# A decode layer on one core: one weight block moved between DMA engines, the order of the last loads, and transposes on VectorE

## The chip, the core and the metric

The kernel runs on one core of a Trainium2 chip. A core has TensorE (matrix multiply, "PE" in the profile; its weight loads are listed apart as "PEld"), VectorE ("DVE"), ScalarE ("ACT"), GpSimd ("POOL") and SyncE ("SP"), which here only issues DMAs. Sixteen DMA engines move data between HBM and the on-chip memory (SBUF). The metric is device time in microseconds; the runs shown of one kernel lie within 0.03% of each other.

## The reference

A decode step for 8 rows `x` (8 x 512, fp32): attention with 32 query heads over 8 cached key/value heads of 4096 positions and head width 128, and a gated MLP, both on the layer-normalised `x`.

```python
xn = layernorm(x)
q = (xn @ wq)                                   # 32 heads of 128
p = softmax(q @ k_cache^T * 128**-0.5)          # each kv head serves 4 query heads
s = (p @ v_cache) @ wo                          # 4096 x 512
z = gelu(xn @ w_in); z1, z2 = z[:, :896], layernorm(z[:, 896:])
g = silu((z1 * (w_sp * z2 + b_sp)) @ w_out)     # w_out: 896 x 512
out = x + s * g
```

Nearly all bytes are the two caches, 134 MB each; the weights are some 22 MB.

## The kernel before

All large data pass through a ring of three SBUF slots of 64 KB in each of 128 partitions (8 MB a slot). SP issues the loads in program order on one queue: the MLP weights and `w_out` as one transfer (`w_mlp`, L59), `wq` (L74), then for every kv head two key halves (`load_k`, L289) and two value halves (`load_v`, L296), each 8 MB and each issued when the slot it goes into has been read for the last time. `x` comes on ACT's queue (L71). The 128 rows of a transfer are shared out over the 16 DMA engines.

The order of work on the engines is that of the program, with small shifts by the build. First the layer norm of `x` (L121 to L129), then the MLP (`mlp()`: its first product L144, its second, with `w_out` in 7 blocks of 128 rows, L185, its gate, L200), the queries (`project_q`, L207 to L219), then per kv head: `scores` (L230, 64 matmuls a half; each shows as two records in the trace), `softmax` (L237 to L267), and per pair of batch rows `values` (L275) with a masked sum on VectorE (L278, L280) and a small matmul `combine` (L284).

In `softmax` the probabilities `p` (128 x 1024) are transposed by TensorE in 8 blocks (L262) and copied by VectorE in 16 pieces into `pT` (L266). `pT` holds zeros beside each row so that two batch rows can share one 32-column group; `values` then has two batch rows for each result, and four results for a head.

The end of the kernel: after the last key half, the last slot is filled with `wo`, which is 32 blocks of 128 x 512 (256 KB each). Blocks 0 to 11 (`WO_EARLY`) go ahead of the last value half, which comes in two parts, and the other 20 follow in the pieces of `WO_PIECES` (L322). `project_o` multiplies blocks 0 to 27 (`FOLDED`) with the heads' results into `part` (L304); `part` is copied to SBUF (L343) and folded into the 128 x 64 output layout by 16 matmul records (L359). The last four blocks go straight into that layout (`direct`, L351): blocks 28 and 29 ahead of the fold, 30 and 31 (from `AHEAD` on) behind it. Two VectorE operations (L363, L364) and the store (L365) end the kernel. `part` and `acc`, the sum in the output layout, are views of the one PSUM tile `sc`.

Of the kernel before, what the change touches and what calls it, by code (L numbers as in the profile page):

```python
# [8 lines left out]
F32 = mybir.dt.float32  # L9
# [13 lines left out]
NB = FH // P  # L23
EPS = 1e-5
# [13 lines left out]
def tile_gqa_gmlp_decode(ctx: ExitStack, tc: tile.TileContext, x, kT, v, wq, wo, w_mlp, out, gate, stored):  # L38
# [18 lines left out]
    n_in, n_out = NK * 2 * FH, NB * D  # L57
# [3 lines left out]
    w_out_sb = mlp_slot[:, n_in:n_in + n_out].rearrange("p (j d) -> p j d", j=NB)  # L61
# [9 lines left out]
    nc.scalar.dma_start(x_sb, x)  # L71
# [16 lines left out]
    for g in range(1, G):  # L88
# [4 lines left out]
    fold = const.tile([P, 2, REP], F32, name="fold")  # L93
    nc.vector.tensor_reduce(fold, same[:, 0, :].rearrange("p (e g r) -> p e r g", e=2, g=G),
                            op=ALU.add, axis=AX.X)
    pT = const.tile([P, J, B, 2, G * REP], F32, name="pT")
    nc.gpsimd.memset(pT, 0.0)  # L97
# [8 lines left out]
    for t in o_ps:  # L106
        nc.vector.memset(t, 0.0)
# [25 lines left out]
    def mlp():  # L133
# [44 lines left out]
        for a in range(2):  # L178
            th = scratch([P, P], "th")
            nc.tensor.transpose(th, u[:, 1, a * P:(a + 1) * P], ident)  # L180
            nc.vector.tensor_copy(hT[:, a, :], th)
        pw = scratch([P, D], "pw")
        for j in range(NB):
            g, a = divmod(j, 2)
            nc.tensor.matmul(pw[R * g:R * (g + 1), :], hT[:, a, R * g:R * (g + 1)], w_out_sb[:, j, :],  # L185
                             start=(a == 0), stop=(a == 1 or j == NB - 1))
# [46 lines left out]
    pT_v = pT.rearrange("p j (i e) f q -> p j i e f q", e=2)  # L233

    def softmax(h):
        m = nm[:, h:h + 1]
        nc.vector.tensor_reduce(m, sc, op=ALU.max, axis=AX.XY, negate=True)  # L237
        p = work.tile([P, J, P], F32, name="p")
        nc.scalar.activation(p.rearrange("p j s -> p (j s)"), sc.rearrange("p c s -> p (c s)"), AF.Exp,  # L239
# [19 lines left out]
        for c in range(2):  # L259
            t = scratch([P, 512], "t")  # L260
            for j in range(4):
                nc.tensor.transpose(t[:, j * P:(j + 1) * P], p[:, 4 * c + j, :], ident)  # L262
            for j in range(4):
                tv = t[:, j * P:(j + 1) * P].rearrange("p (g i e r) -> p i e g r", g=G, i=B // 2, e=2)
                for e in range(2):
                    nc.vector.tensor_copy(  # L266
                        pT_v[:, 4 * c + j, :, e, e].rearrange("p i (g r) -> p i g r", g=G), tv[:, :, e])  # L267

    def values(i, v_pair):
        o = o_ps[i % 2]  # L270
        of = o.rearrange("p g d -> p (g d)")
        for j in range(J):
            c = j % G
            for e in range(2):
                nc.tensor.matmul(of[R * c:R * (c + 1), :], pT[:, j, 2 * i + e].rearrange("p e q -> p (e q)"),  # L275
                                 v_pair[:, e, j], start=(j < G and e == 0), stop=(j >= J - G and e == 1))
# [3 lines left out]
        nc.vector.tensor_reduce(o_sb, o_all.rearrange("p g d -> p d g"), op=ALU.add, axis=AX.X)  # L280
        return o_sb

    def combine(i, o_sb, po):
        nc.tensor.matmul(po[:, i * 2 * REP:(i + 1) * 2 * REP], o_sb, fold.rearrange("p e r -> p (e r)"),  # L284
                         start=True, stop=True)
# [13 lines left out]
    part, acc = sc[:, 0, :], sc[:, 1, :W]  # L299
# [10 lines left out]
    for h in range(HKV):  # L310
        for half in range(2):
            scores(h, half, load_k(h, half))
        softmax(h)
        po = po_ps[:, h % 2]
        for half in range(2):
            last = h == HKV - 1 and half == 1
            if last:
                wo_slot = slot()
                nc.sync.dma_start(wo_slot[:, :WO_EARLY * D], wo[:, :WO_EARLY * D])
                v_sb = load_v(h, half, 2)  # L320
                for lo, hi in WO_PIECES:
                    nc.sync.dma_start(wo_slot[:, lo * D:hi * D], wo[:, lo * D:hi * D])  # L322
# [10 lines left out]
        combine(B // 2 - 1, o_prev, po)  # L333
        po_t = po.rearrange("p (b r) -> p r b", r=REP)
        if h < HKV - 1:
            nc.vector.tensor_copy(oT[:, h], po_t)
        else:
            for a in range(2):
                nc.vector.tensor_copy(oT_last[:, :, a, a * B:(a + 1) * B], po_t)
# [6 lines left out]
    def direct(lo, hi):  # L346
        for m in range(lo, hi):
            for a in range(2):
                for g in range(G):
                    c = (2 * g + a) * W  # L350
                    nc.tensor.matmul(acc[R * g:R * g + OUT_ROWS, :], oT_last[:, m - FOLDED, a, :],  # L351
# [53 lines left out]
```

## Time and profile before

| what | value |
|---|---|
| median of 3 runs | 681.76 us (681.75 to 681.92) |
| the profiled execution | 682.35 us |
| its span | 680.8 us |
| data moved in | 290.80 MB, 427 GB/s over the span |
| PE, DVE, ACT, POOL busy | 54%, 18%, 2%, 1% of the span |
| mean granted TensorE clock | 0.727 |

The span is what the profile's times count from and to; the device time of the same execution is 1.55 us more. A line of the profile's timeline gives the start, the duration of the run of instructions, the engine, the source line, the operation, the tiles (out<-in), and in brackets the engine's idle time before it with what ended it. "SPq" and "ACTq" are the queues that issue DMAs. A view by stretches gives for each stretch of time the busy time and the number of instructions of each engine, the granted share of TensorE's clock, the share of time in which the 16 DMA engines were busy, and the rate.

### The profile page before, as it was taken

How to read it: one execution, taken by the hardware profiler on the slowest of the kernel's cores; microseconds unless marked ns; L12 is line 12 of the kernel's file. 1: busy time of each engine (PE TensorE's matmuls, PEld its weight loads, DVE VectorE, ACT ScalarE, POOL GpSimd, SP SyncE). 2: the span in 40 equal slices, each digit the busy share in tenths (PEclk: the TensorE clock that was granted, in tenths of full speed). 3: DMA queues.
4: the chain of work that ended last, by engine and by line, in shares of the span. 5: the costliest groups of instructions: out<-in, count | busy, mean ns of one | idle time of the engine just before them, and what ended most of it. 6: DMA issues, size and time to landing. Idle time of an engine off the chain costs nothing.

```text
span 680.8 us, 5589 instructions
## 1 busy us (share of the span) xinstructions
PE 368.2 (54%) x2488; PEld 119.5 (18%) x2488; DVE 121.6 (18%) x376; ACT 13.4 (2%) x27; POOL 5.6 (1%) x13
## 2 busy tenths in 40 slices
PE   0485564447555454546654354556654455555667
PEld 0121121112111121112211021111311121111212
DVE  2431031202220032201320032201311032200321
ACT  0000000000000000000000000000000000000000
POOL 2000000000000000000000000000000000000000
PEclk9777656777876666787776667877765677887677
DMA  9999999999999999999999999999999999999996
GB/s 390 431 432 432 432 431 432 443 432 450 440 431 429 431 428 431 431 428 431 432 432 439 443 436 431 428 431 432 439 425 450 435 428 440 443 432 431 401 426 262
DMA packets 6231, 291.18 MB, mean 428 GB/s; under 512 B 824, under 2 KB 824, under 8 KB 1344
## 3 DMA queue, kind: packets, MB, share of 16 engines
q1 hardware_dynamic: 6048, 290.79, 98.8%
q8 instruction: 19, 0.31, 0.2%
q10 hardware_dynamic: 160, 0.05, 0.0%
q14 instruction: 4, 0.03, 0.0%
HBM read 290.80 MB, written 0.03 MB: 427 GB/s over the span
## 4 chain that ended last, share of the span: by engine, by line
DMA 76%; PE 17%; issue 4%; DVE 1%; POOL 1%; another core or an unknown queue 1%; POOLq 0%; SPq 0%
DMA slot<-in_v 40%; DMA slot<-in_kT 36%; PE o_ps L275 8%; PE sc L230 7%; PE scr L207 1%; PE sc L304 0%; POOL qz L84 0%; PE sc L351 0%; DVE o_sb L280 0%; POOL pT L97 0%; DVE o_all L343 0%; DVE o_all L278 0%; DVE q_sb L210 0%; DVE slot L188 0%
## 5 line engine op out<-in xcount | busy, mean ns | idle before, releaser
L230 PE MATMUL sc<-slot,qz 128*32 128x512 f32 x1024 | 149.6, 749 | 141.6 <-DMA slot<-in_kT 141.6
L275 PE MATMUL o_ps<-slot,pT 128*32 128x512 f32 x1024 | 152.5, 758 | 82.9 <-DMA slot<-in_v 82.9
L230 PEld LDWEIGHTS sc<-slot,qz 128*32 128x32 f32 x1024 | 36.3, 134 | 248.6 <-DMA slot<-in_kT 144.7
L275 PEld LDWEIGHTS o_ps<-slot,pT 128*32 128x32 f32 x1024 | 45.1, 132 | 178.8 <-issue 114.0
L237 DVE TENSOR_REDUCE nm<-sc 128x1 f32<-128x1024 f32 x8 | 9.8, 1225 | 287.9 <-PE sc L230 287.9
L278 DVE TENSOR_TENSOR o_all<-o_ps,diag 128x512 f32<-128x512 f32 x32 | 22.1, 692 | 203.2 <-PE o_ps L275 203.2
L280 DVE TENSOR_REDUCE o_sb<-o_all 128x128 f32<-128x512 f32 x32 | 34.2, 1070 | 1.1
L284 PE MATMUL po_ps<-fold,o_sb 128*128 128x8 f32 x64 | 12.5, 268 | 24.1 <-DVE o_sb L280 24.1
L262 PE MATMUL scr<-ident,p 128*128 128x128 f32 x64 | 15.2, 418 | 10.7 <-DVE p L258 10.7
L239 ACT ACTIVATE p<-sc,nm 128x1024 f32<-128x1024 f32 x8 | 8.9, 1114 | 578.1 <-DVE nm L237 578.1
L266 DVE COPY pT<-scr 128x64 f32<-128x64 f32 x128 | 17.6, 216 | 9.9 <-PE scr L262 9.9
L284 PEld LDWEIGHTS po_ps<-fold,o_sb 128*128 128x128 f32 x64 | 9.6, 188 | 40.6 <-DVE o_sb L280 27.2
L262 PEld LDWEIGHTS scr<-ident,p 128*128 128x128 f32 x64 | 12.3, 217 | 11.1 <-issue 11.1
L144 PE MATMUL scr<-slot,xnT 128*32 128x512 f32 (+1 forms) x32 | 6.6, 904 | 9.6 <-DMA slot<-in_w_mlp 9.6
L207 PE MATMUL scr<-slot,xnT 128*32 128x512 f32 x64 | 8.9, 707 | 0.0
L242 PE MATMUL scr<-ident,nm 128*1 128x128 f32 x8 | 2.2, 270 | 10.9 <-DVE nm L237 10.9
L304 PE MATMUL sc<-slot,oT 128*8 128x512 f32 x56 | 7.4, 593 | 0.0
L255 PE MATMUL scr<-wl,same 128*128 128x1 f32 x16 | 3.8, 309 | 6.2 <-DVE wl L253 6.2
L258 DVE TENSOR_SCALAR p<-p,w 128x1024 f32<-128x1024 f32 x8 | 6.0, 753 | 0.3
L159 PE MATMUL scr<-part_sum,same 128*128 128x1 f32 x4 | 1.1, 348 | 7.0 <-DVE part_sum L157 7.0
L219 DVE COPY qz<-scr 128x4 f32<-128x4 f32 x64 | 4.6, 152 | 1.5 <-PE scr L213 1.5
L248 PE MATMUL scr<-ident,full 1*128 1x1 f32 x8 | 1.6, 205 | 5.7 <-DVE full L246 5.7
(87 smaller groups left out, 65.1 us busy)
## 6 DMA issues: line engine op xcount, KB each, us to landing
slot<-in_v SPq DMA_DIRECT2D x2, 4096.0 KB, 32.0
slot<-in_w_mlp SPq DMA_DIRECT2D x1, 5440.0 KB, 15.4
slot<-in_wo SPq DMA_DIRECT2D x1, 3072.0 KB, 38.2
slot<-in_wo SPq DMA_DIRECT2D x1, 2048.0 KB, 41.0
slot<-in_wo SPq DMA_DIRECT2D x1, 1536.0 KB, 44.5
slot<-in_wo SPq DMA_DIRECT2D x2, 512.0 KB, 45.2
slot<-in_wo SPq DMA_DIRECT2D x2, 256.0 KB, 35.2
slot<-in_kT SPq DMA_DIRECT2D x16, 48.9
```

Of the source, the lines that this page charges most:

```text
L144: nc.tensor.matmul(pz_v[R * g:R * (g + 1), :, :n], xnT[:, k, :], w_in_v[:, k, :, lo:lo + n], start=(k == 0), stop=(k == NK - 1))
L207: nc.tensor.matmul(pq[R * g:R * (g + 1), :], xnT[:, k, :], wq_sb[:, k, lo:lo + REP * DH], start=(k == 0), stop=(k == NK - 1))
L230: nc.tensor.matmul(sc[R * g:R * (g + 1), c, :], qz[:, h, b * R:(b + 1) * R], k_sb[:, i, c, g, :], start=(b == 0), stop=(b == B - 1))
L237: nc.vector.tensor_reduce(m, sc, op=ALU.max, axis=AX.XY, negate=True)
L239: nc.scalar.activation(p.rearrange("p j s -> p (j s)"), sc.rearrange("p c s -> p (c s)"), AF.Exp, bias=m, accum_out=l[:, h:h + 1])
L262: nc.tensor.transpose(t[:, j * P:(j + 1) * P], p[:, 4 * c + j, :], ident)
L266: nc.vector.tensor_copy(pT_v[:, 4 * c + j, :, e, e].rearrange("p i (g r) -> p i g r", g=G), tv[:, :, e])
L275: nc.tensor.matmul(of[R * c:R * (c + 1), :], pT[:, j, 2 * i + e].rearrange("p e q -> p (e q)"), v_pair[:, e, j], start=(j < G and e == 0), ...
L278: nc.vector.tensor_mul(o_all, o, diag[:, :, None].to_broadcast([P, G, DH]))
L280: nc.vector.tensor_reduce(o_sb, o_all.rearrange("p g d -> p d g"), op=ALU.add, axis=AX.X)
L284: nc.tensor.matmul(po[:, i * 2 * REP:(i + 1) * 2 * REP], o_sb, fold.rearrange("p e r -> p (e r)"), start=True, stop=True)
L304: nc.tensor.matmul(part[R * r:R * r + B, :], oT[:, h, r, :], wo_sb[:, m, :], start=(m < REP), stop=(m >= FOLDED - REP))
```

## The change

Six things are changed together.

- Block 1 of the 7 blocks of `w_out` leaves `w_mlp` and comes in two transfers of its own (`EXTRA`), as rows of 8 KB: 20 rows that spread over 5 DMA engines (0 to 4) and 12 rows that spread over 3 (0 to 2). The source has a fifth row after every four that is not read, so that its outer size stays 5 and 3. In `mlp()` the moved block is multiplied in 8 smaller matmuls, 4 chunks each of 20 and of 12 rows, from a transposed copy `hE` made for them (4 small TensorE transposes, 3 VectorE copies, one memset). The 14 products are dealt over the four column groups.
- `x` is loaded by SP, behind `w_mlp`, no longer by ACT at the start.
- In `softmax` one VectorE transpose takes the place of the 8 TensorE transposes and 16 copies; `pT` has no zeros any more (its memset goes), and the key cache is laid out on the host in an order that fits.
- `values` takes 4 batch rows for each result instead of 2, one 16-row strip each (2 in the last half); so masked sums and `combine` matmuls fall from 32 to 17.
- 8 instead of 12 `wo` blocks go ahead of the last value half; the other 24 follow in 8 pieces.
- `project_o` takes 29 blocks instead of 28, `direct` the last 3; `acc` has a PSUM tile of its own.

```diff
+EXTRA = [(0, 5), (R, 3)]
+CHUNKS = 4
+MOVED = 1
-WO_EARLY = 12
-WO_PIECES = [(12, 20), (20, 26), (26, 28), (28, 30), (30, 31), (31, 32)]
-FOLDED = HKV * REP - REP
-AHEAD = FOLDED + 2
+WO_EARLY = 8
+WO_PIECES = [(8, 14), (14, 19), (19, 23), (23, 26), (26, 29), (29, 30), (30, 31), (31, 32)]
+FOLDED = HKV * REP - 3
+AHEAD = FOLDED + 1
...
-    nc.scalar.dma_start(x_sb, x)
+    nc.sync.dma_start(x_sb, x)
+    w_ex = from_slot(P, CHUNKS * D).rearrange("p (c d) -> p c d", c=CHUNKS)
+    for (lo, k), src in zip(EXTRA, (w_ex0, w_ex1)):
+        nc.sync.dma_start(w_ex[lo:lo + 4 * k], src[:, :4])
...
+    acc = ps_fix.tile([P, W], F32, name="acc")
...
+            if j == MOVED:
+                for i, (lo, k) in enumerate(EXTRA):
+                    parts[g - i] += [(hE[lo:lo + 4 * k, c, :], w_ex[lo:lo + 4 * k, c, :]) for c in range(CHUNKS)]
+            else:
+                parts[g].append((hT[:, a, R * g:R * (g + 1)], w_out_sb[:, j - (j > MOVED), :]))
+        for i in range(max(map(len, parts))):
+            for g in range(G):
+                if i < len(parts[g]):
+                    nc.tensor.matmul(pw[R * g:R * (g + 1), :], *parts[g][i],
+                                     start=(i == 0), stop=(i == len(parts[g]) - 1))
...
-        for c in range(2):
-            t = scratch([P, 512], "t")
-            for j in range(4):
-                nc.tensor.transpose(t[:, j * P:(j + 1) * P], p[:, 4 * c + j, :], ident)
-            for j in range(4):
-                tv = t[:, j * P:(j + 1) * P].rearrange("p (g i e r) -> p i e g r", g=G, i=B // 2, e=2)
-                for e in range(2):
-                    nc.vector.tensor_copy(
-                        pT_v[:, 4 * c + j, :, e, e].rearrange("p i (g r) -> p i g r", g=G), tv[:, :, e])
+        pT = work.tile([P, J, B, G, REP], F32, name="pT")
+        nc.vector.transpose(pT.rearrange("p j b g r -> p j g b r"),
+                            p.rearrange("p (j g b r) -> p j g b r", j=J, g=G, b=B))
...
+        rows = HALF // n
         for j in range(J):
-            c = j % G
-            for e in range(2):
-                nc.tensor.matmul(of[R * c:R * (c + 1), :], pT[:, j, 2 * i + e].rearrange("p e q -> p (e q)"),
-                                 v_pair[:, e, j], start=(j < G and e == 0), stop=(j >= J - G and e == 1))
+            for i in range(n):
+                c = i * rows + j % rows
+                nc.tensor.matmul(of[R * c:R * c + G * REP, :], pT[:, j, b0 + i],
+                                 v_sb[:, i, j], start=(j < rows), stop=(j >= J - rows))
...
-            for n in range(HALF // 2):
-                i = half * (HALF // 2) + n
-                o_sb = values(i, v_sb[:, 2 * n:2 * n + 2])
-                if i > 0:
-                    combine(i - 1, o_prev, po)
-                o_prev = o_sb
+            n = 2 if last else HALF
+            for i in range(0, HALF, n):
+                done = values(half * HALF + i, n, pT, v_sb[:, i:i + n])
+                if half or i:
+                    combine(*o_prev, po)
+                o_prev = done
```

More of the change, by code (lines that the diff above doesn't have):

```diff
@@ L105, in tile_gqa_gmlp_decode @@
     po_ps = ps_fix.tile([P, 2, B * REP], F32, name="po_ps")
-    for t in o_ps:
+    acc = ps_fix.tile([P, W], F32, name="acc")
+    for t in [acc, *o_ps]:
         nc.vector.memset(t, 0.0)
@@ L280, in values, with combine @@
         nc.vector.tensor_reduce(o_sb, o_all.rearrange("p g d -> p d g"), op=ALU.add, axis=AX.X)
-        return o_sb
-    def combine(i, o_sb, po):
-        nc.tensor.matmul(po[:, i * 2 * REP:(i + 1) * 2 * REP], o_sb, fold.rearrange("p e r -> p (e r)"),
+        return b0, n, o_sb
+    def combine(b0, n, o_sb, po):
+        f = fold if n == HALF else fold_last
+        nc.tensor.matmul(po[:, b0 * REP:(b0 + n) * REP], o_sb, f.rearrange("p i r -> p (i r)"),
                          start=True, stop=True)
@@ L297, in load_v @@
         return t.rearrange("p (i j e) -> p i j e", i=HALF, j=J)
-    part, acc = sc[:, 0, :], sc[:, 1, :W]
+    part = sc[:, 0, :]
     def project_o(lo, hi):
```

80 lines of the change are left out of this document (54 added, 26 removed).

## The prediction

> **What bounds the kernel now.** I read the page first, then the chain that ended last.
>
> ```profile
> span 680.8 us, 5589 instructions
> ...
> PE 368.2 (54%) x2488; PEld 119.5 (18%) x2488; DVE 121.6 (18%) x376; ACT 13.4 (2%) x27; POOL 5.6 (1%) x13
> ...
> GB/s 390 431 432 432 432 431 432 443 432 450 440 431 429 431 428 431 431 428 431 432 432 439 443 436 431 428 431 432 439 425 450 435 428 440 443 432 431 401 426 262
> ...
> q1 hardware_dynamic: 6048, 290.79, 98.8%
> q8 instruction: 19, 0.31, 0.2%
> q10 hardware_dynamic: 160, 0.05, 0.0%
> q14 instruction: 4, 0.03, 0.0%
> ...
> DMA 76%; PE 17%; issue 4%; DVE 1%; POOL 1%; another core or an unknown queue 1%; POOLq 0%; SPq 0%
> ```
>
> The load queue q1 fills 98.8% of the 16 engines' time at some 432 GB/s, in every slice but the last. So compute only matters where it follows the last loads.
>
> The chain and the timeline show that end:
>
> ```profile
> 628.46 36.68 DMA slot<-in_v
> ...
> 665.18 6.39 PE L275 MATMUL o_ps<-slot,pT 128*32 128x512 f32 x32 [1.24 <-DMA slot<-in_v]
> ...
> 673.51 0.39 PE L284 MATMUL po_ps<-fold,o_sb 128*128 128x8 f32 x2 [0.25 <-DVE o_sb L280]
> ...
> 673.83 2.75 PE L304 MATMUL sc<-slot,oT 128*8 128x512 f32 x22
> ...
> 676.64 0.69 DVE L343 COPY o_all<-sc 128x512 f32<-128x512 f32 x1 [2.42 <-PE sc L304]
> ...
> 677.44 0.64 PE L351 MATMUL sc<-slot,oT_last 128*16 128x64 f32 x32 [0.85 <-DVE o_all L343]
> ...
> 677.88 0.42 PE L359 MATMUL sc<-o_all,pick 128*16 128x64 f32 x16
> ...
> 678.10 0.64 PE L351 MATMUL sc<-slot,oT_last 128*16 128x64 f32 x32
> 678.80 0.23 DVE L363 TENSOR_TENSOR gate<-sc,gate 128x64 f32<-128x64 f32 x1 [1.47 <-PE sc L351]
> ...
> 679.32 0.38 ACTq L365 DMA_DIRECT2D out<-gate  x1
> ```
>
> From the landing of the last value part (628.46 + 36.68 = 665.1) to the store at 679.32 it is compute: 14.1 us. The wo pieces land beside it:
>
> ```profile
> L322 SPq DMA_DIRECT2D slot<-in_wo x6: 328/421/432, 628.9 to 645.8; - x6
> ...
> DMA to landing us min/median/max: 31.8/41.0/45.2
> ```
>
> The last piece, issued at 645.8, took the shortest time, 31.8, and landed at 677.6: 1.7 us before the store, and before block 31 was due. Then the stretches of the tail (second column from the right: share of the 16 DMA engines that is busy; before it the granted clock):
>
> ```profile
> 669.00:670.00 1.00, 1.00 (x8) 0.22 (x4) 0.00 (x0) 0.00 (x0) 0.00 (x0) 0.50 1.01 418
> 671.40:672.40 1.00, 1.00 (x13) 0.28 (x6) 0.69 (x1) 0.00 (x0) 0.00 (x0) 1.00 0.97 391
> 672.90:675.10 2.20, 1.95 (x15) 0.89 (x18) 0.85 (x3) 0.00 (x0) 0.00 (x0) 1.00 0.56 226
> 675.80:676.60 0.80, 0.79 (x7) 0.00 (x0) 0.00 (x0) 0.00 (x0) 0.00 (x0) 1.00 0.19 74
> ```
>
> 0.56 is 9 engines of 16, 0.19 is 3. So seven engines have finished by about 672.6, six more by about 675.5, three work until about 677.2. Each carried the same share of q1, so something else took their time. The 19 fetches of q8 fit: 2 x 2488 PE instructions make 262 a fetch, so it is TensorE's code, and 19 dealt in turn over eight engines gives three fetches to three of them and two to five. With the engine of q14's code that is the 3, the 6 and the 7 that have none. A fetch then costs its engine some 1.4 us (672.6 to 675.5 is two, 675.5 to 677.2 one; 0.2% of 16 spans over 19 is 1.1, rounded).
>
> **The change, part by part.**
>
> Chunks. At 432 GB/s one 256 KB block takes 0.61 us, 16 KB on each engine. Without it engines 5 to 15 end 0.61 us sooner. Engines 3 and 4 get 32 KB, net +0.61; engines 0 to 2 get 64 KB, net +1.82. If these are among the seven early ones they end near 674.4, well before the late three. No view names engines, so this is bounded from both sides: -0.61 on the last landing, or +1.82. I take -0.61: of 16 engines seven are early, a round of eight fetching engines that are neighbours leaves the other eight as neighbours too, and five low ones fit among them. That puts the last piece at 677.6 - 0.6 = 677.0.
>
> That short transfers stay on fewer engines shows in q10's 160 packets: 128 + 16 are the store's rows and completions on 16 engines, the other 16 are x's 8 rows on 8.
>
> Code. The edit removes 128 PE instructions with the 64 transposes, 60 with 15 of the 32 `combine` (four each), 28 at the end, and adds 36 in the MLP: 4976 becomes about 4796, at 262 a fetch 18.3 instead of 19. The nineteenth fetch falls to the very end or away. Two engines keep three, so the last landing gains little: 0 if one of these two was the last, and I take 0.1, with 0.2 as the other end.
>
> Order of wo. Four blocks behind the last value part instead of ahead bring it 4 x 0.61 = 2.43 us sooner, with the block moved away 3.04: PE starts at 662.1, and with the same 8.33 us to `combine` (673.51 - 665.18) that comes at 670.5. The wo bytes all lie before the end as they did, so the last landing does not gain from this. Two more pieces of wo and the two of chunks: 20 blocks in six pieces took 677.6 - 665.1 = 12.5 us, where their bytes take 12.1, so a transfer costs at most 0.07 of its own; two more in the tail are 0.1, less than what the roundings leave, and I take 0. What is late next is the piece of blocks 26 to 28. It lands three blocks before the end, 677.0 - 3 x 0.61 = 675.1, less the 0.1: 675.05. From there:
>
> ```profile
> L304 PE MATMUL sc<-slot,oT x56: 592/592/597, 648.3 to 676.0; 128*8 128x512 f32 x56
> ```
>
> Four records run side by side, one a column group; the 22 in 2.75 us are six rounds, (2.75 - 0.59) / 5 = 0.43 apart. Three blocks are two rounds, 0.43 + 0.59 = 1.02. Then the copy L343 with its wait, 0.06 + 0.69. From its end (677.33) to the store it took 1.99 us with 80 small records, 1.30 us together; block 29 can now go ahead of the copy, because `acc` has its own tile, so 48 are left: 0.5 to 0.4 us less, 1.55. Sum: 675.05 + 0.05 + 1.02 + 0.75 + 1.55 = 678.4 against 679.32: 0.9 us sooner.
>
> Two other paths end before that. The last piece at 676.9 needs block 31's 16 records (about 0.6) and the last 0.52 from L363 to the store: 678.0. And after `combine` at 670.5 some 16 blocks remain, eight rounds, 4.0 us: 674.5, covered by the wait for blocks 26 to 28 with 0.5 us to spare. `combine` itself stands behind whatever `project_o` work the build puts before it; those need blocks 8 to 13, landed by 666.
>
> Softmax.
>
> ```profile
> 628.09 1.23 DVE L237 TENSOR_REDUCE nm<-sc 128x1 f32<-128x1024 f32 x1 [37.84 <-PE sc L230]
> ...
> 632.10 0.75 DVE L258 TENSOR_SCALAR p<-p,w 128x1024 f32<-128x1024 f32 x1
> ...
> 633.95 2.19 DVE L266 COPY pT<-scr 128x64 f32<-128x64 f32 x16 [1.10 <-PE scr L262]
> ...
> 638.39 9.61 PE L275 MATMUL o_ps<-slot,pT 128*32 128x512 f32 x64 [3.63 <-DMA slot<-in_v]
> ```
>
> No transpose on VectorE shows before. At 1024 elements the nearest rows are 0.75 (L258) and 1.23 (L237); I take 1.23, above it perhaps four times that, 4.9. It replaces 3.3 us (632.85 to 636.14). Even 4.9 stays under the 3.3 + the wait for values. In all heads this costs and gains nothing, as do fewer sums and `combine` matmuls: q1's next transfer has long been issued.
>
> Start.
>
> ```profile
> 3.01 0.68 DVE L121 BATCH_NORM_STATS2 st<-slot 8x6 f32<-8x512 f32 x1 [0.95 <-DMA slot<-in_x]
> ...
> 6.71 0.19 DVE L129 COPY xnT<-scr 128x32 f32<-128x32 f32 x1
> ...
> 16.29 6.55 PE L144 MATMUL scr<-slot,xnT 128*32 128x512 f32 x32 [9.62 <-DMA slot<-in_w_mlp]
> ...
> 34.22 3.85 PE L185 MATMUL scr<-slot 128*32 128x512 f32 x14 [0.17 <-DVE slot L181]
> ...
> 41.02 0.22 DVE L200 TENSOR_TENSOR gate<-scr,slot 128x64 f32<-128x64 f32 x1
> ```
>
> The same start on SP's queue, and the time from issue to landing of its first two transfers:
>
> ```profile
> 1.64 40.01 SPq L289 DMA_DIRECT2D slot<-in_kT  x2
> ...
> slot<-in_w_mlp SPq DMA_DIRECT2D x1, 5440.0 KB, 15.4
> ...
> slot<-in_wq SPq DMA_DIRECT2D x1, 34.3
> ```
>
> `x` now lands with the MLP weights, near 15.7 (16.29 - 0.61), and the layer norm's 3.9 us (3.01 to 6.90) no longer hide beside them: L144 starts at 19.6, +3.3. L185 had 4 records in its fullest column group in 3.85 us, 0.96 each; now there are 10, +5.8. The extra transposes and copies, about 0.6. So the gate, 41.24, ends 9.7 us later, and on SP the second key half, which waits for that slot until 41.65, goes out at 51.4, all later loads behind it in order. It is due when the queue runs dry: wq landed by 1.64 + 34.3 = 35.9, the first key half 19.4 later, 55.3; less 2.5 for a transfer's start (w_mlp took 15.4 where 5440 KB take 12.9), 52.8. Covered by 1.4 us, with every record at its cold price. Beyond that point each microsecond would stretch the whole run. `x` away from the front leaves the first transfer alone at the start: between 0 and 0.9 of those 2.5 us; I take 0, because it is not told how much of them is x's.
>
> **Sum.** The store 0.9 us sooner: the profiled execution, 682.35 with span 680.8, becomes 681.45 with span 679.9. It lay 0.6 above the median of 681.76 of the runs, so that median becomes 680.85.
>
> **The rivals.**
>
> The chunks hit late engines. For: no view names engines. Then the last landing is 677.6 + 1.82 = 679.4, blocks 26 to 28 land at 677.5, and the store follows 3.4 later at 680.9: 683.3, slower. It decides once the loaded engines would end after 676.5, that is if one of 0 to 2 has two fetches or more.
>
> TensorE's clock falls in the tail.
>
> ```profile
> 660.60:663.80 3.20, 1.26 (x14) 0.35 (x6) 1.73 (x2) 0.00 (x0) 0.00 (x0) 1.00 0.96 415
> 664.00:667.00 3.00, 1.82 (x12) 0.55 (x16) 0.00 (x0) 0.00 (x0) 0.00 (x0) 0.50 0.99 422
> 661.65:663.50 1.85, 0.00 (x0) 0.00 (x0) 1.73 (x2) 0.00 (x0) 0.00 (x0) 1.00 1.05 452
> ```
>
> It halved after 3.2 us with 1.26 of work in them. In the new tail PE waits for pieces between 671 and 675 with some 2 us of work in 3.2, so it should stay up. If it halves before blocks 26 to 28 land, the two rounds cost 0.9 more and the 48 records 0.7: 682.45, within 0.2% of before. The Trainium skill ("TensorE: Matmul & The Clock Gate", Part 1) has it fall after an idle window of about 3.4 us, and by that it would stay up here for certain; the trace, with 1.85 us idle before a fall, is less kind.
>
> The MLP overruns 52.8: each microsecond over is one more, so 683.35 with 2.5 over. For: only 1.4 us of cover. Against: that cover is counted with dear records.
>
> The start gains. With x gone from the front, 0.5 to 0.9 us of the lost 2.5 comes back for all engines: 680.1.
>
> Every transfer pays a price of its own. The row above leaves at most 0.07 each, four more are 0.3: 681.15, still the forecast's own range. The Trainium skill ("DMA: Bandwidth & Descriptors", Anatomy of one DMA) fits some 2.0 us a transfer beside its bytes; four of them in series would make 8 us and 689. The trace does not agree for queued ones, as six in 12.5 us show.
>
> **How the numbers follow.** Forecast 0.51 (own range 680.3 to 681.3); start gains 0.20; clock 0.12; late engines 0.10; MLP overrun 0.05; a price for each transfer 0.02. 0.2% is 1.4 us, about what a measurement of this kernel can tell from no change: 680.4 and 683.1. Faster: 0.20 and 0.08 of the forecast, 0.28. Slower: the late engines and the MLP, 0.15. Same: 0.57. The range takes in the start and the clock and leaves out those two: 680.0 to 682.9.
>
> **What would show it.** DMA share in the tail: seven engines no longer done four microseconds before the rest; last landing near 677. A wait of L304 for in_wo near 675. L275's last run from 662. L121 near 15.7, the gate by 51, and no gap in q1 near 54. One transpose of about 1.2 us a head. The prediction is wrong if the last wo landing is after 677.6, if SP's second key load comes after 52.8, or if PE runs L304 at half clock.

## The result, and the profile after

The changed kernel takes 682.99 us (median of 14 runs, 682.25 to 683.78) against 681.92 for the kernel before beside it (14 runs, 681.66 to 682.67): the ratio is 1.0015, with a 95% interval of 1.0008 to 1.0022. It is 1.07 us slower. That is within the 0.2% that the prediction set as its bound, but clear of no change, and outside the predicted range (680.0 to 682.9; 680.85 forecast). The three runs shown ahead of the prediction lay within 0.03% of each other; these 14 of the same kernel spread over 1.0 us, 0.15%. One slow execution, the profiled one of e5 at 804.39 us, is left out below; the ten others of e5 lie between 681.78 and 682.24.

The page of the changed kernel (span, busy time, rate in 40 slices, queues, the chain's shares). Its execution took 682.8 us, near the median:

```profile
span 681.3 us, 5241 instructions
...
PE 351.6 (52%) x2398; PEld 92.2 (14%) x2398; DVE 88.0 (13%) x233; ACT 13.4 (2%) x27; POOL 3.9 (1%) x12
...
GB/s 378 435 446 413 432 442 432 431 432 435 432 439 432 435 440 431 431 428 431 428 435 432 435 439 444 439 432 431 432 431 432 431 431 440 440 435 440 406 419 272
...
q1 hardware_dynamic: 6392, 290.80, 98.9%
q8 instruction: 19, 0.31, 0.2%
...
q14 instruction: 3, 0.02, 0.0%
...
DMA 79%; PE 17%; issue 3%; DVE 1%; POOLq 0%; POOL 0%
```

DMA bounds it as before. TensorE and VectorE do less (the transposes, copies and sums are gone: 368.2 to 351.6 us and 121.6 to 88.0), and that brings nothing. Two slices are low that were not: the first (390 to 378) and the fourth (432 to 413, 51 to 68 us). So the start comes first. Its timeline (start, duration, engine, line, tiles, and in brackets the idle time before it and its releaser), and SP's queue:

```profile
15.89 0.67 DVE L128 BATCH_NORM_STATS2 st<-slot 8x6 f32<-8x512 f32 x1
...
19.14 5.72 PE L151 MATMUL scr<-slot,xnT 128*32 128x512 f32 x32 [0.29 <-DVE xnT L136]
...
36.39 12.73 PE L218 MATMUL scr<-slot 128*32 128x512 f32 x28
...
52.05 0.22 DVE L233 TENSOR_TENSOR gate<-scr,slot 128x64 f32<-128x64 f32 x1
```

```profile
3.77 48.91 SPq L320 DMA_DIRECT2D slot<-in_kT  x2
60.94 8.80 SPq L327 DMA_DIRECT2D slot<-in_v  x2
```

The layer norm of `x` now begins at 15.89, and the first MLP product at 19.14, 2.85 later than before. The `w_out` products take 12.73 us instead of 3.85. The gate ends at 52.27, and only then, at 52.35 (its issue ends at 3.77 + 48.91 = 52.68), SP can send the second key half; before that was at 41.3.

The tail of the changed kernel, a line of the chain that ended last and the timeline behind it:

```profile
637.82 38.12 DMA slot<-in_wo
```

```profile
675.98 1.04 PE L335 MATMUL sc<-slot,oT 128*8 128x512 f32 x6 [0.71 <-DMA slot<-in_wo]
676.72 0.52 PE L382 MATMUL acc<-slot,oT_last 128*16 128x64 f32 x16
677.10 0.69 DVE L374 COPY o_all<-sc 128x512 f32<-128x512 f32 x1 [4.98 <-PE sc L335]
677.85 0.42 PE L390 MATMUL acc<-o_all,pick 128*16 128x64 f32 x16 [0.61 <-DVE o_all L374]
678.08 0.63 PE L382 MATMUL acc<-slot,oT_last 128*16 128x64 f32 x32
...
679.30 0.37 ACTq L396 DMA_DIRECT2D out<-gate  x1
```

The piece of blocks 26 to 28 lands at 637.82 + 38.12 = 675.94, and the store follows 3.36 later, at 679.30. The prediction had 675.05 and 3.35. TensorE waits there for DMA, as forecast, but for a piece that is 0.9 late.

How the store fared stands in its issue row, first of the changed kernel, then of the kernel before (in both from the view of the store's own line):

```profile
DMA to landing us min/median/max: 2.0/2.0/2.0
```

```profile
DMA to landing us min/median/max: 1.5/1.5/1.5
```

In the trace's packet records the nineteenth fetch of TensorE's code (16 KB) starts at 678.91 and occupies one engine for 1.31 us; the store's share on 15 engines completes between 680.62 and 680.79, and on one at 681.30.

### The profile page after: what moved, and what is told of

It reads as the page before. It is cut to its first block, busy times and chain, and to the rows that moved or that the text cites. A ratio compares the mean times of both kernels' runs of the same rounds, so it can differ in the third digit from the quotient of the medians.

```text
span 681.3 us, 5241 instructions
## 1 busy us (share of the span) xinstructions
PE 351.6 (52%) x2398; PEld 92.2 (14%) x2398; DVE 88.0 (13%) x233; ACT 13.4 (2%) x27; POOL 3.9 (1%) x12
## 4 chain that ended last, share of the span: by engine, by line
DMA 79%; PE 17%; issue 3%; DVE 1%; POOLq 0%; POOL 0%
DMA slot<-in_v 43%; DMA slot<-in_kT 29%; PE o_ps L305 7%; PE sc L263 6%; DMA slot<-in_wo 6%; DMA slot<-in_w_mlp 2%; PE scr L218 2%; PE scr L240 1%; DVE q_sb L243 0%; PE scr L246 0%; PE sc L335 0%; DVE o_all L374 0%; DVE slot L221 0%; PE scr L225 0%; POOLq L440 0%
## 5 line engine op out<-in xcount | busy, mean ns | idle before, releaser
L263 PE MATMUL sc<-slot,qz 128*32 128x512 f32 x1024 | 146.9, 738 | 133.0 <-DMA slot<-in_kT 133.0
L305 PE MATMUL o_ps<-slot,pT 128*16 128x512 f32 x1024 | 149.5, 749 | 111.2 <-DMA slot<-in_v 111.2
L263 PEld LDWEIGHTS sc<-slot,qz 128*32 128x32 f32 x1024 | 37.8, 132 | 235.8 <-issue 150.5
L305 PEld LDWEIGHTS o_ps<-slot,pT 128*16 128x16 f32 x1024 | 33.1, 114 | 213.2 <-issue 151.8
L308 DVE TENSOR_TENSOR o_all<-o_ps,diag 128x512 f32<-128x512 f32 x17 | 11.8, 692 | 246.3 <-PE o_ps L305 246.3
L315 PE MATMUL po_ps<-fold,o_sb 128*128 128x16 f32 x30 | 6.0, 276 | 26.8 <-DVE o_sb L310 26.8
L310 DVE TENSOR_REDUCE o_sb<-o_all 128x128 f32<-128x512 f32 x17 | 17.8, 1046 | 0.6
L218 PE MATMUL scr<-slot 128*32 128x512 f32 (+2 forms) x28 | 12.7, 1058 | 0.0
L315 PEld LDWEIGHTS po_ps<-fold,o_sb 128*128 128x128 f32 x30 | 4.6, 191 | 40.6 <-DVE o_sb L310 40.6
L291 DVE STREAM_TRANSPOSE pT<-p 128x1024 f32<-128x1024 f32 x8 | 10.0, 1246 | 0.3
```

The lines of the kernel that those rows point to most:

```text
L218: nc.tensor.matmul(pw[R * g:R * (g + 1), :], *parts[g][i], start=(i == 0), stop=(i == len(parts[g]) - 1))
L263: nc.tensor.matmul(sc[R * g:R * (g + 1), c, :], qz[:, h, b * R:(b + 1) * R], k_sb[:, i, c, g, :], start=(b == 0), stop=(b == B - 1))
L291: nc.vector.transpose(pT.rearrange("p j b g r -> p j g b r"), p.rearrange("p (j g b r) -> p j g b r", j=J, g=G, b=B))
L305: nc.tensor.matmul(of[R * c:R * c + G * REP, :], pT[:, j, b0 + i], v_sb[:, i, j], start=(j < rows), stop=(j >= J - rows))
L315: nc.tensor.matmul(po[:, b0 * REP:(b0 + n) * REP], o_sb, f.rearrange("p i r -> p (i r)"), start=True, stop=True)
```

## The experiments

Landings and completions below that have no row of their own are the completion events in the traces. Each group shared its runs of the kernel before (27 to 33 of them, medians 681.92, 681.81, 681.98 and 681.96 for e1 to e4, e5 to e8, e9 to e12, and e13 to e15), and each difference is to its own group's median. One ratio has an interval of about 0.0009 to each side, 0.6 us. So most single differences below are suggestions; what is called shown rests on intervals that do not meet.

**e1, x first.** Only the place of x's load is undone.

```diff
-    nc.sync.dma_start(x_sb, x)
+    nc.scalar.dma_start(x_sb, x)   # ahead of w_mlp's landing, as before
```

> The changed kernel with x loaded at the start on ACT's queue again. Theory 'late issue': the second key half went out at 52.35, when the load queue had nothing left, and the restart cost every late engine about 1.0 us. Here the layer norm is done early, the MLP ends 2.9 us sooner, the second key half goes out near 49.5, the load queue goes through without slow rows, the last value part lands near 662.2 (663.2 in the changed kernel), the store is issued near 678.4 (679.3): 0.9 us less than the changed kernel. Rival 'the chunks': short rows on few engines disturb the stream by themselves; then the last value part still lands near 663.2 and the store stays near 679.3. If the code fetch that came at 678.9 still falls on the store, its landing takes 2.0 us after the issue, otherwise 1.5.

681.72 us (11 runs), ratio 0.9994 [0.9985, 1.0002], against 1.0015 [1.0008, 1.0022] for the whole change: 1.27 us less, and the intervals do not meet. The second key half is issued at 49.82 (SP's row for the first two key halves; its end, 3.38 + 46.78, lies 0.33 behind the start of the second issue):

```profile
3.38 46.78 SPq L320 DMA_DIRECT2D slot<-in_kT  x2
```

So x behind the weights costs more than the whole loss, and the rest of the change is about neutral.

**e2, the kernel before with a late slot.** The copy of the `w_out` products is done 18 times, which holds back nothing but the gate and the slot.

```diff
-        nc.vector.tensor_copy(y_sb, pw)
+        for _ in range(18):
+            nc.vector.tensor_copy(y_sb, pw)
```

> The kernel before with one VectorE copy in the MLP done 18 times instead of once, which lets the MLP end some 12 us later and nothing else. Theory 'late issue': the second key half goes out near 53.4, the queue runs dry, the last value part lands 1.0 to 1.6 us later than 665.1, the store follows it, the time grows by 1.0 to 1.6 us. Rival 'the chunks': without chunks there is nothing to lose, the time stays within 0.2 us of before.

682.69, ratio 1.0009 [1.0000, 1.0018], second key half issued at 53.76 instead of 41.3. A late issue alone costs some 0.77 us in the kernel before, less than expected; the interval just touches no change.

**e3, no chunks, x first.** The wo order and the VectorE transposes, with `w_out` in one piece.

> The changed kernel with w_out whole in the MLP weights and x at the start, so with the order of wo, the transposes and the values of the change alone. Both theories: the second key half goes out near 42, the last value part lands near 662.7, blocks 26 to 28 near 675.7, the store is issued near 679.1, 0.2 us sooner than before. 'Late issue' has e1 0.6 us faster than this (the chunks' worth); 'the chunks' has e1 slower than this by 0.2 us or more. 36 PE instructions fewer than in the changed kernel: if the code fetch at the end goes with them, the store lands 1.5 us after its issue, and the kernel is 0.2 us faster than before.

682.20, ratio 1.0002 [0.9994, 1.0011]. The expected gain of 0.2 us did not show: the median is 0.28 above the kernel before, and the interval allows at most 0.4 of gain.

**e4, chunks alone**, in the kernel before.

> The kernel before with the chunks alone; x at the start. The chunks' products make the MLP 9.2 us longer (from the end of L183 to the gate 17.1 us in the changed kernel, 7.9 before), so the second key half goes out near 50.9. Theory 'late issue': that is about in time; the last value part lands 0.6 us sooner, 664.5, the store is issued near 678.7, 0.6 us less than before. Rival 'the chunks': no gain or a loss of 0.4 us. A result between says that the issue has to come earlier than 50.9.

681.53, ratio 0.9994 [0.9985, 1.0003], 0.39 less than before, not clear of no change. In its trace the last wo piece lands at 676.69 (677.58 and, in e12, 677.43 before). The direction is the predicted one, the size in the medians smaller; in this one execution the store still goes out at 678.76, as in e12 (678.75), because it follows the copy of `part`.

**e5, the wo order alone**, in the kernel before.

```diff
-WO_EARLY = 12
-FOLDED = HKV * REP - REP
+WO_EARLY = 8     # and the eight pieces of the change
+FOLDED = HKV * REP - 3
+    acc = ps_fix.tile([P, W], F32, name="acc")
```

> The kernel before with the wo order of the change alone: 8 blocks ahead of the last V tile, the eight later pieces, 29 blocks folded, acc in a bank of its own; values, transposes, x and w_out as before. The prediction's term: V 0.61 sooner and the end bound by the piece of blocks 26 to 28, which took 0.9 off the end against the profiled run of before; then some 681.3 against 681.92, with 0.3 of it open because that profiled run may not be a typical one. Rival: the run with the order, the transposes and x first was 0.28 slower than before, and if that is the order, this comes to 682.2. Third: the end is bound by the last of the bytes either way, and the order is worth nothing: 681.8 to 682.0.

681.91, ratio 1.0001 [0.9992, 1.0010]: no change. The 681.3 that the prediction's term gave would be a ratio of 0.9993, at the very edge of that interval; the 0.9 itself (0.9987) is outside.

**e6, the transposes alone**, with `acc` in its own tile.

> The kernel before with the VectorE transposes and the values over four batches alone (wo order, w_out and x as before). All of it lies beside the DMA, so 681.7 to 682.1, the same as before. Rival: the 0.28 that the run without chunks lost comes from here (fewer PE instructions put the code fetches at other places of the stream, with none in the last 12 us): then 682.2. If the theory of the store and the code fetch holds there is no fetch beside the store here, and the store takes the 1.5 us that it takes in the trace of before.

681.61, ratio 0.9996 [0.9987, 1.0005]. They cost nothing that shows, as predicted.

**e7, wide rows.** The changed kernel, x late, with 8 rows and 2 chunks for each engine instead of 4 and 4; it should have shortened the MLP.

```diff
-EXTRA = [(0, 5), (R, 3)]
-CHUNKS = 4
+EXTRA = [(0, 5), (2 * R, 3)]
+CHUNKS = 2
+ROWS = 8
```

> The changed kernel, x behind w_mlp as in it, with the moved block in 8 rows and 2 chunks for each engine instead of 4 rows and 4 chunks: the same 32 KB for each engine. The w_out products go from 28 records at 1.06 us to 20, some 8.5 us less 4 ns, so about 3.5 to 4 us off the stage and the gate at 48.0 to 48.8 instead of 52.27; the second key half is issued at 48.1 to 48.9. Theory (the overrun of the MLP costs the time): the whole 1.27 us that x first brought comes back, 681.6 to 681.9. Rival (x behind the weights costs by another way, say by its place on the queue): 682.8 to 683.2, as the changed kernel. The nineteenth code fetch still lies beside the store in both cases.

684.10 (7 runs), ratio 1.0029 [1.0018, 1.0040]: slower still. The edit missed its aim, since the 20 records take as long as the 28 did, and the weights landed 1.1 us later. A line of its view by line, and SP's row for the key halves in its timeline:

```profile
L220 PE MATMUL scr<-slot 128*32 128x512 f32 (+2 forms) x20 | 13.0, 1060 | 0.0
```

```profile
3.78 50.77 SPq L322 DMA_DIRECT2D slot<-in_kT  x2
```

The second key half went out at 54.23, 1.88 later than in the changed kernel, and the time rose by 1.1. This is no further point for a late issue, because the load queue itself was late. The packet records show why: the 64 KB packets that started at 14.7 to 16.6, beside the chunks, took up to 4.1 us, where 2.42 is usual. The first ten engines then complete the first key half at 55.68 to 56.12, against 53.74 to 54.38 in the changed kernel, so the second was sent 1.4 us ahead of the first of these completions in both. The added 1.1 us fits the slow packets at the start; that was not tested by itself. Why fewer records did not help, the changed kernel's own view by line with the forms apart shows (after the bar: busy time, mean ns of one):

```profile
L218 PE MATMUL scr<-slot 12*32 12x512 f32 x8 | 7.2, 1056 | 0.0
L218 PE MATMUL scr<-slot 20*32 20x512 f32 x8 | 7.2, 1056 | 0.0
L218 PE MATMUL scr<-slot 128*32 128x512 f32 x12 | 5.8, 1062 | 0.0
```

The 28 records start in 14 rounds, 0.84 to 0.99 apart: three of 128 rows side by side in two rounds, two of them in two, one in two, and in eight rounds one of 20 rows beside one of 12. Short products never ran beside those of 128 rows. In e7 the records of 40 and 24 rows did not even run beside each other, and 20 made 14 rounds again.

**e8, the fetch moved.** x first, and 72 idle-time transposes on TensorE behind the fourth softmax, so that the nineteenth code fetch comes earlier.

> The changed kernel with x first, and 72 transposes of the identity more on TensorE behind the fourth softmax, where it waits for DMA: they change no result, and bring its instructions to the number of the kernel before, so that the nineteenth code fetch comes some 150 instructions sooner, at 660 to 672 us, and no longer beside the store. Theory (the fetch holds the store 0.5 to 0.8 us): 681.72 less that, 680.9 to 681.2, and the store lands 1.5 us after its issue. Rival (the fetch delays another engine's bytes as much wherever it falls in the last 20 us, or the collision is of the profiled run alone): 681.6 to 681.9.

681.50, ratio 0.9995 [0.9986, 1.0004], 0.22 less than e1 in the median (0.11 against its own group). The fetch came at 672.8, and the store landed in 1.5 us. The half microsecond that a single execution with the fetch beside the store shows is not seen in full between medians; 0.1 to 0.2 of it may be there, and these runs cannot tell that from nothing.

**e9, x first, but late again.** The copy done five times in e1's kernel.

> The changed kernel with x first, and the copy of the w_out products to SBUF done five times instead of once, 4 x 0.69 us more ahead of the second key half: issued at 52.4 to 52.7, as late as in the changed kernel (52.35), where x first alone has 49.82. Theory (the late issue costs the time, whatever makes it late): the 1.27 us come back, 682.8 to 683.3. Rival (x's place on the queue costs by itself): 681.5 to 681.9, as x first.

682.85, ratio 1.0016 [1.0007, 1.0025], with the second key half at 52.79. Its row on SP's queue, where the first issue is 0.1 later than in e1:

```profile
3.47 49.65 SPq L321 DMA_DIRECT2D slot<-in_kT  x2
```

The loss is back although x is first: against e1 the intervals do not meet. x's place on the queue is not what costs.

**e10, few products.** The changed kernel, x late, with one of the four chunks multiplied; three quarters of one `w_out` block are left out of the sum, and all bytes are still loaded.

```diff
-... for c in range(CHUNKS)]
+... for c in range(KEPT)]     # KEPT = 1
```

> The changed kernel, x behind w_mlp, with the products of the first of the four chunks alone, so three quarters of one w_out block are left out of the sum (all bytes are still loaded). The w_out products go from seven steps of two passes to four, 5.5 us less: the gate at 46.8 and the second key half issued at 46.9. Theory (late issue): 681.5 to 681.9, as x first. Rival (x's place costs): 682.7 to 683.2, as the changed kernel.

681.47, ratio 0.9993 [0.9984, 1.0002], against 1.0015 [1.0008, 1.0022]. Its products and the issue (timeline, and SP's queue):

```profile
36.51 5.63 PE L219 MATMUL scr<-slot 128*32 128x512 f32 x16
...
45.38 0.33 SPq L321 DMA_DIRECT2D slot<-in_kT  x1
```

7.1 us less in the products instead of the expected 5.5, the issue at 45.38, and the whole loss is gone although x is late. (Here no code fetch lies beside the store, which lands in 1.5 us instead of 2.0; but e1, whose store takes 2.3, is as fast.) With e9 this shows the cause from both sides: the time is lost because the second key half is sent too late, whatever makes it late.

The traces say where it is lost. At the landing of that second key half the eight engines that are first complete at 74.02 to 74.65 in the changed kernel and at 73.13 to 73.57 in e10. At the last V part the same gap is still there: seven engines complete at 661.65 to 661.97 against 660.55 to 660.84.

The packet records show in what form. In e10, at the place where the second key half begins, thirteen 64 KB packets start between 53.25 and 53.90 and take 2.42 us each. In the changed kernel the engines reach it at nearly the same time: twelve packets start between 53.42 and 54.37, but eleven of them take 2.77 to 3.66 us. Against e10 that is some 0.4 us of later start and some 0.8 us of longer packets, and the next packets take 2.42 again. So little of the loss is an empty queue; most of it is slow first packets of a load that was sent only a microsecond ahead of them. In e9 and e2, both sent late too, such packets take up to 3.2 us. Why they are slow, no run here shows.

**e11, the old wo order.** x first, chunks and transposes, but 12 blocks early, six pieces and 28 folded blocks.

> The changed kernel with x first and the wo order of before (12 blocks ahead of the last V tile, six pieces, 28 blocks folded): the chunks and the VectorE transposes without the order. If the three parts add and the order is worth nothing, 681.4 to 681.7 (the chunks alone stood 0.39 under before, the transposes alone 0.20 under). If the order brings the 0.9 that the prediction took, 682.3 or more. There is no code fetch beside the store.

680.99 us, ratio 0.9986 [0.9978, 0.9995]: faster than the kernel before and than the changed one, 0.73 less than e1, which differs from it in the order alone. So the order seems to cost here; the two intervals overlap, and the tail has to show it:

```profile
675.52 0.69 DVE L375 COPY o_all<-sc 128x512 f32<-128x512 f32 x1 [3.01 <-PE sc L335]
675.75 0.64 PE L383 MATMUL acc<-slot,oT_last 128*16 128x64 f32 x32 [0.27 <-DMA slot<-in_wo]
676.27 0.42 PE L391 MATMUL acc<-o_all,pick 128*16 128x64 f32 x16
676.51 0.84 PE L383 MATMUL acc<-slot,oT_last 128*16 128x64 f32 x32
...
677.94 0.37 ACTq L397 DMA_DIRECT2D out<-gate  x1
```

The fold (L391) is done before the last piece lands at 676.89, and the store follows that landing by 1.05. In the changed kernel the last piece lands at 677.82 and the store follows by 1.48, because the fold waits longer: blocks 26 to 28 land only 1.88 before the last block and need 3.36 from there.

**e12, the kernel before again**, unchanged, for a second profile.

> The kernel before, unchanged, to see how far one profiled execution lies from another: the ratio 1.0000 within its interval of 0.001, and, if the profiled execution of before was a slow one, the last V part landing some 0.3 to 0.7 sooner than its 665.13 and the store issued some 0.4 sooner than its 679.32. Rival: both within 0.2 of those, and the term of 0.9 for the order was lost in the tail itself.

681.92, ratio 1.0000 [0.9991, 1.0009]. Its profiled execution took 681.77, where the first one had 682.35:

```profile
676.07 0.69 DVE L343 COPY o_all<-sc 128x512 f32<-128x512 f32 x1 [2.87 <-PE sc L304]
676.86 0.64 PE L351 MATMUL sc<-slot,oT_last 128*16 128x64 f32 x32 [0.84 <-DVE o_all L343]
...
678.75 0.37 ACTq L365 DMA_DIRECT2D out<-gate  x1
```

The last V part lands at 665.15, as in the first (665.13), but the store goes out at 678.75 instead of 679.32.

What of the wo order costs 0.73 was still open, so its parts were taken apart.

**e13, V sooner, 28 folded.** e1 with 8 blocks early, pieces that end at block 28, and 28 folded.

```diff
-WO_PIECES = [..., (23, 26), (26, 29), (29, 30), (30, 31), (31, 32)]
-FOLDED = HKV * REP - 3
+WO_PIECES = [..., (23, 26), (26, 28), (28, 30), (30, 31), (31, 32)]
+FOLDED = HKV * REP - REP
```

> The changed kernel with x first and 8 blocks of wo ahead of the last V tile (V sooner, as in the change), but with 28 blocks folded as before, in pieces of which one ends at block 28. The theory of the tail: the store is issued at the later of (the landing of the last piece + 1.05) and (the landing of the last folded piece + 3.35). Here the last folded piece lands 2.4 to 2.5 ahead of the last one, so the last piece decides, + 1.05, as in the run with the old order: 680.9 to 681.2. Rival (V sooner costs something by itself): 681.4 to 681.8.

681.17, ratio 0.9988 [0.9980, 0.9997]. Its store, at 678.23, follows the last landing (677.19) by 1.04:

```profile
675.83 0.69 DVE L375 COPY o_all<-sc 128x512 f32<-128x512 f32 x1 [4.87 <-PE sc L335]
...
678.23 0.38 ACTq L397 DMA_DIRECT2D out<-gate  x1
```

**e14, V late, 29 folded.** e1 with the old 12 blocks early, pieces (12, 20), (20, 26), (26, 29), (29, 30), (30, 31), (31, 32), and 29 folded.

> The changed kernel with x first, 12 blocks ahead of the last V tile (V late, as before), and 29 blocks folded with a piece of blocks 26 to 28, as in the change. By the theory of the tail that piece lands 1.87 ahead of the last, so the store is issued 1.48 behind the last landing instead of 1.05: 681.3 to 681.7, as x first with the whole order. Rival (it is the early V that costs): 680.9 to 681.1.

681.69, ratio 0.9994 [0.9985, 1.0003]. Blocks 26 to 28 land at 674.90, the last at 676.75:

```profile
676.06 0.69 DVE L374 COPY o_all<-sc 128x512 f32<-128x512 f32 x1 [3.46 <-PE sc L335]
...
678.26 0.38 ACTq L396 DMA_DIRECT2D out<-gate  x1
```

That is 3.36 and 1.51. In the eleven tails with the new values and `acc` in its own tile (the changed kernel, e1, e3, e6 to e11, e13, e14) the store goes out within 0.02 of the later of (last folded piece + 3.36) and (last piece + 1.05). The two medians fall where this rule put them. Folding 29 blocks with the piece of blocks 26 to 28 accounts for 0.4 to 0.5 in these rows; between the medians it is 0.52 (e14 against e13), with intervals that overlap. V sooner (e13 against e11, 0.18) neither gains nor costs anything that shows.

**e15, acc in its own tile**, alone in the kernel before.

> The kernel before, with acc in a PSUM bank of its own instead of the second half of sc, and nothing else. In both profiles of before the direct products of blocks 28 and 29 start 0.10 behind the end of the copy of part, and the last store is issued 1.32 and 1.74 behind the last landing; with acc by itself they stand ahead of the copy, and the last landing + 1.05 decides or the copy's end + 1.50: 0.2 to 0.3 sooner, 681.6 to 681.7. Rival: the copy's start (by V and the values) decides, and nothing changes, 681.8 to 682.0.

681.67, ratio 0.9996 [0.9987, 1.0005]. In e12's rows the direct products start 0.10 behind the copy of `part`, on the shared tile, and the store follows the copy's end by 1.99. Here it is 1.50:

```profile
676.52 0.75 PE L352 MATMUL acc<-slot,oT_last 128*16 128x64 f32 x32
676.88 0.69 DVE L344 COPY o_all<-sc 128x512 f32<-128x512 f32 x1 [2.41 <-PE sc L305]
...
679.08 0.38 ACTq L366 DMA_DIRECT2D out<-gate  x1
```

The half microsecond behind the copy is shown by the rows; that it shortens the whole (0.29 in the medians) is not, within 0.6, and in this execution the store itself goes out later than in e12.

## Why the prediction was wrong

**Start: the step that failed.** It said the second key half would go out at 51.4 and was due at 52.8, "covered by 1.4 us, with every record at its cold price". Two terms were off. (The 51.4 continues from 41.65, the end of the issue before. Like for like that end came at 52.68, 1.3 later. Both lie before the 52.8 that the prediction named as its sign of being wrong, so that sign could not show it: the due time itself was wrong. The sign that did show was the last wo landing, 677.82 where 677.6 was the limit.)

- The `w_out` products were priced by the fullest column group, 10 records of 0.96, 9.65 us. They took 14 rounds, 12.73. It supposed that records of other column groups always run side by side, as four do in `project_o`; those of 20 and 12 rows ran only beside each other, not beside those of 128 rows. On this point "TensorEngine Tiling (Array Packing)" of the Trainium skill (Restrictions and Gotchas) says that different row tiles cannot access the same PSUM bank at once. The trace does not agree with that: records of 12 and of 20 rows, on row tiles 1 and 0, start 7 ns apart (at 44.514 and 44.520, for one), and both add into the one tile `pw` (128 x 512). What keeps the 128-row records apart from the short ones, no run here shows.
- The due time was too late. Taking a microsecond for each microsecond over, as the prediction did, the medians put it at 52.35 - 1.27 = 51.1 in the changed kernel and 52.79 - 1.07 = 51.7 in e9 (the losses against e1, each first taken against its own group's before). For the kernel without chunks e2 gives 53.76 - 0.77 = 53.0, close to the predicted 52.8, but with 0.6 open to each side. About 0.6 of the difference is the change's own gain: the eleven engines without chunks have 0.61 us less to carry, so they run dry that much sooner. The first ten complete the first key half at 53.74 to 54.38 in the changed kernel; in e12 thirteen do at 54.31 to 54.82. The prediction counted these 0.61 us at the end and forgot them here. Another 0.5 is a slip: its 35.9 for the landing of `wq` adds 34.3 to 1.64, which is the issue of the first key half; `wq` went out at 1.17 and landed at 35.48. What remains, 0.7 at most, is open. And a microsecond late did not stretch the run as an empty queue does: most of the loss lies in the slow first packets (e10).

So the rival "the MLP overruns" (0.05, 683.35) was the right one in kind, and was held too unlikely. That its figure lies near the measured 682.99 is luck: it stands on 2.5 us over and on the 0.9 of the order, where about 1 over and no gain were measured. The start's other terms held: x lands with the weights, and the first product starts at 19.14 for a forecast 19.6.

**Order of wo: the mechanism right, the gain not.** V landed two microseconds sooner (663.17 for 665.13; predicted 662.1), the end moved to the piece of blocks 26 to 28, and from it to the store took 3.36 for a predicted 3.35. But the -0.9 had two faults. It was measured from an execution whose store lay 0.57 later than that of e12: the prediction saw that this execution lay 0.6 above the median, carried the 0.6 over as an offset, and yet let the edit remove it. And it held the two bounds of the tail side by side (678.4 by the folded piece, 678.0 by the last one) without asking what the old cut of pieces would give once the transposes and the separate `acc` were in: there the last piece decides, 0.4 to 0.5 sooner than with 29 folded (e11, e13, e14).

**Code: missed.** "The nineteenth fetch falls to the very end or away" was right, but its price was looked for at the last landing alone. At the very end it lies beside the store: 2.0 us to land for 1.5 in this execution.

**The sum, with the measured terms.** From e12's store at 678.75: the predicted 678.4 is -0.35; the late start moves the folded piece by 675.94 - 675.05 = +0.89; the store takes +0.5. That is +1.04, against 682.8 - 681.77 = 1.03 between the two executions and 1.07 between the medians. That e10, where the load is sent in time, has the folded piece at 674.93, close to the forecast, speaks for putting the +0.89 down to the late start. That the medians agree as well is partly luck, since e8 did not show the 0.5 between medians.

**What held.** Chunks: the loaded engines did not end last. With the chunks alone (e4) the last piece lands 0.7 to 0.9 sooner than in the two profiles of before, for a predicted 0.6, where the rival had it 1.8 later. No record names an engine, so which of the early ones carry the chunks stays open. A code fetch: worked out at 1.4 us for its engine, and that is what the packet records give (see the end). Softmax: the transpose was taken at 1.23, and takes 1.246, hidden:

```profile
L291 DVE STREAM_TRANSPOSE pT<-p 128x1024 f32<-128x1024 f32 x8 | 10.0, 1246 | 0.3
```

The clock: the rival that it falls in the tail is out. Stretches of the changed kernel's tail (third column from the right: granted clock):

```profile
671.00:675.00 4.00, 3.80 (x29) 1.07 (x28) 0.64 (x4) 0.00 (x0) 0.00 (x0) 1.00 0.90 366
675.90:677.10 1.20, 1.12 (x22) 0.48 (x22) 0.00 (x0) 0.00 (x0) 0.00 (x0) 1.00 0.21 79
677.80:678.80 1.00, 0.86 (x48) 0.69 (x48) 0.02 (x1) 0.00 (x0) 0.00 (x0) 1.00 0.00 0
```

It stayed at 1.00. Start gains: `w_mlp` lands at 15.76 in the changed kernel, and at 15.91 and 16.19 in e1 and e4, which load the same bytes with x first. In e10, with x late as in the changed kernel, it lands at 16.05, so the differences are no more than executions differ by.

The 2.0 us a transfer that the prediction takes from the Trainium skill ("DMA: Bandwidth & Descriptors", Anatomy of one DMA) is there a fit for transfers issued by GpSimd; the loads here are issued by SP. The six in 12.5 us stand against it either way, and it had no part in the sum.

## What to carry to other kernels

In a kernel bound by one load queue, work out for every load that waits for a slot when the queue would run dry without it, and take from that due time whatever the change itself takes off the loads ahead; a side computation that holds a slot can be off the critical path by 11 us before an edit (issued at 41.3, due near 53) and on it after. A load that is sent only just in time can still be late: here its first packets were slow. At the end, write the finish as the later of a few sums (landing of each late piece + the work behind it) and cut the pieces so that the last one decides. Before a gain is taken off a profiled execution, ask whether that execution is itself late, and in which row.

## What was not expected

- A fetch of 16 KB of TensorE's code takes its DMA engine 1.43 us in the stream: 0.88 to 0.97 for its own packet, and most of the 64 KB packets right behind one take 2.88 to 2.97 instead of 2.42. One that falls beside the last store goes with a store that lands later, by 0.5 us in the changed kernel and 0.8 in e1 (2.0 and 2.3 us to land, 1.5 without). It has to fall close: where the fetch starts 0.2 to 0.4 us ahead of the store's issue (the changed kernel, e1, e6, e9, e14) the store takes 1.6 to 2.3 us, where it starts over 0.6 ahead (e11, e13) it takes 1.5. Which instruction count puts a fetch there is arithmetic: e8 moved it with 72 more transposes, whose work costs nothing.
- A product of 12 or 20 rows took as long as one of 128 (1056 and 1062 ns at half clock), and ran at best beside another short one, so cutting one block into eight small products made 14 rounds of records where the seven blocks had taken 3.85 us.
- The version with all of the change but the wo order, and x first (e11), beats both kernels: 680.99 us, ratio 0.9986 [0.9978, 0.9995] to the kernel before.
